# A planned order of steps, replanned from step 560 on: order, buffers and the engines of 50 steps

## The chip, the cores and the metric

One core of a Trainium2 chip runs the whole program. The metric is the device time of one execution in microseconds (us), as the median of three runs. The engines are named as in the profile: PE (matrix products), PEld (PE's weight loads, which overlap the products), DVE (vector engine), ACT (scalar engine), POOL (GpSimd) and SP (which issues the transfers).

## The reference, cut to what matters

```python
# q, k, v: (4, 4, 1088, 32); S1, S2: (8, 32); w1, w2: (128, 1024); w3: (1024, 1024); w_out: (1024, 128)
phi(x) = outer product of (S1 x) and (S2 x), 64 features for each position
kv  = einsum('bhsf,bhsd->bhfd', phi(k), v);  z = sum over s of phi(k)
att = einsum('bhsf,bhfd->bhsd', phi(q), kv) / (einsum('bhsf,bhf->bhs', phi(q), z) + 1e-6)
x   = att, heads side by side: (4352, 128)
out = ((x @ w1) * (x @ w2)) @ w3 @ w_out
```

## The kernel before, in words

The kernel is written as 1181 named steps, each a few instructions on one engine. A list, `ORDER`, gives the order in which they are issued; every engine works its own instructions off strictly in that order. Four further tables belong to the plan: `SLOTS` says which of the buffers of a kind each allocation takes (kind "b" is the eight PSUM banks; "l", "m" and "s" are SBUF buffers of three sizes; "raw" are the three biggest), `POOL` names the elementwise steps that run on POOL and not on DVE (the function `on`), `CPV` the copies that run on DVE and not on ACT (the function `cp`).

What the step names mean:

- `k0.*` to `k3.*`: the four batches of keys; `k3.kv*` are the value sums of the last batch that is taken up, of which the step that closes them is `k3.kvr`. `k2.kv*` are those of the third batch.
- `q0.*` to `q3.*`: half batches of 512 queries of batches 0 and 1. `q4.*` and `q6.*`: the 1024 queries of batches 2 and 3, as one chain each (`q_wide`, L1308 and below). `qr.*`: the 64 last positions of every batch. A chain runs `tr max l2 l1 rm A0 C0 C1 At Ct sm st sh sl sc al p01 p2 p12 dn de rc bs na nb nm nr ne nn phi pT x xT`. `phi0` and `phi1` (L1509) are the two halves of the feature product, 128x1024 each; `pT0` and `pT1` (L1517) turn them; `x` (L1527) is PE's product of the turned features with the key sums, 32 small products that write four PSUM banks; `xT0` to `xT3` (L1540) copy these banks out.
- `w*` and `f*`: the weights are unpacked, and w3 and w_out are folded into one matrix `w3o` (L534).
- `g0.*` to `g3.*`: the feed-forward layers for batches 0 and 1, eight slices each: `a` and `b` (L1799, L1809) are products with w1 and w2, `c` copies `a` out, `m` (L1815) multiplies, `o` (L1835) is the product with `w3o`. `oT` (L1842) takes the output bank out, `st` issues the transfers to the output.
- `h4.*` and `h6.*`: the feed-forward layers for batches 2 and 3, in which seven half-size products replace eight (`seven`, L1636 and below). For each of four slices and two halves `a`, `b`: `1` to `7` (L1673) are the products, `c d e i` (L1680) copies, `f g h` (L1685) sums with a bank. `m11 m12 m22` (L1707) and `m21` (L1712) multiply, `T1` to `T4` (L1727 to L1742) form differences, `P1` to `P7` (L1759) are the second products, `k1` to `k9` (L1767 to L1785) join them. `s1` to `s4` and `v.*`, `o.*` form the sums of the inputs and of the weights that these products need.
- `gr.*`: the feed-forward layer for the 256 left-over positions, PE L1799, L1809 and L1824.

Around the change the order was: while PE works through the `o` products of `g0` to `g3`, which depend on nothing that is still to come, DVE, POOL and ACT carry the chains `q4`, `q6` and `qr`; PE takes up `q4.x`, `q6.x` and `qr.x` between these products. Then come `h4`, `h6` and `gr`, whose products each wait for buffers and results of the other engines.

The rule by which a step finds its engine and its buffer:

```python
    def on(name):
        return pool if name in POOL else act if name in ACTS else dve

    def cp(name):
        return dve.tensor_copy if name in CPV else act.copy
...
        if tag in taken:
            return pool.tile(shape, dtype, tag=f"{tag}.{next(taken[tag])}", bufs=1, name=name)
```

Of the kernel before, what the change touches and what calls it, by code (L numbers as in the profile page):

```python
# [45 lines left out]

# [64 lines left out]
g3.5b q6.sl w10.a1 q6.sc q4.dn qr.At g3.5c q4.de f5.t q4.rc g1.0o g1.1o q4.na q4.bs q4.nb f2.m q4.nm q4.nr qr.sm q6.al
q6.p01 q6.p2 g0.0o g0.1o q6.p12 f2.o g0.2o g0.6o k2.kqt g0.3o q4.ne g3.5m q4.nn q6.dn k2.kq f5.m f5.o g3.7b g3.2b
g1.6o g0.5o g0.4o w10.a0 qr.st f7.t f7.m g3.2a q4.phi0 q4.phi1 qr.sh qr.sl qr.sc f7.o q4.pT0 g3.2c q4.pT1 g2.5o g0.7o
g0.oT g3.2m g3.3o g2.3o q4.x q4.xT2 q6.de qr.p01 q6.rc q4.xT0 q6.bs q6.nb q6.na g2.2o g2.7o qr.al q6.nm q6.nr q6.ne
q6.nn v.1 q4.xT1 q6.phi0 q6.phi1 g1.4o o.S3 q4.xT3 g1.2o q6.pT0 g3.5o g3.7m q6.pT1 g1.3o q6.x qr.p2 q6.xT2 qr.p12
qr.dn qr.de g3.1o g1.7o g3.6o g2.1o qr.rc qr.bs q6.xT3 g1.5o q6.xT0 h4.s1 h4.s3 q6.xT1 q6.ns g3.7o g3.2o qr.phi0
qr.pT0 g1.oT qr.x h4.0b5 h4.0a1 qr.xT0 h4.1a1 g2.oT g2.st h4.0b2 g3.oT h4.0a5 h4.0b1 h4.0bd h4.1b1 h4.0ac h4.s2 h4.s4
h4.1ac v.2 h4.0a6 h4.0bc h4.0bh h4.0ae o.S1 h6.s1 h4.0a2 h4.0ah h4.0b3 h4.1b2 o.S2 o.S4 h4.0ad h4.1a6 h6.s2 h4.0a7
h4.0m11 h4.0b6 h4.1a5 g3.st h4.1bc h4.1b6 h4.1ae h4.1bh v.4 h4.0ag h4.0be h4.0bf h4.1b5 h4.0a3 h4.0af h4.0b7 h4.1a7
h4.1be h4.1b7 h4.1ad h4.0a4 h4.0m12 h4.1a2 h4.0bg h4.1bd h4.1b3 h4.1a3 h4.0m22 h4.0b4 h4.1ag h4.2b1 h4.0ai h4.2a1  # L120
h4.1bf h4.2bc h4.2b2 h4.1ah h4.1a4 h4.2a2 h4.2ac h4.1bg h4.1af h4.1m12 h4.1m22 h4.1b4 h4.3b1 h4.2a6 h4.1ai h4.0m21
g1.st h4.2b5 h4.2ae h4.3a1 h4.2bh h4.1m11 h4.2ah h4.1m21 h4.3bc h4.1T1 h4.2m11 h4.3ac h4.2b6 h4.2be h4.2bd h4.0T1
h4.2a5 h4.2ad h4.3a2 h4.3b2 h4.3bh h4.3b6 h4.2a7 h4.2b7 h4.0T3 h4.3a6 h4.3ae h4.2ag h4.2b3 h4.3ah h4.3be h4.2a3 h4.3a5
h4.3ad h4.3b5 h4.3bd h4.2bg h4.2a4 h4.3b7 h4.3a7 h4.1T3 h4.2af h6.1b1 h4.2bf h4.3m11 h4.3a3 h4.2m22 h4.3bg h4.2b4
h4.2ai h4.3ag h4.2m12 h4.3b3 h6.0a1 h4.2m21 h6.0ac h4.3af h4.3a4 h4.1T2 h6.1bc h4.3b4 h6.1a1 h6.0b1 h6.0a6 h4.3ai
h4.3m21 h6.1b6 h4.3bf h4.2T1 h6.1ac h4.0P7 h4.2P1 h4.1P7 h4.0T2 h4.0P1 h4.0T4 h4.1P2 h4.3T1 h4.3m22 h4.1P5 h4.0P4
h6.0bc h4.2P2 h4.0P2 h4.3P5 h4.3m12 h4.2P5 h4.1P6 h4.2T2 h4.2P6 h4.0P5 h4.2T3 h4.1P1 h4.3T3 h4.3P7 h4.2P7 h4.3P1
h4.3T2 h4.3T4 h4.3P6 h4.2T4 h4.2P4 h6.0ae h4.0P6 h4.3P4 h4.1T4 h6.s3 h4.1P4 h4.k1 h4.k3 h4.3P2 h4.k2 h4.0P3 h4.3P3
h4.2P3 h4.k4 h4.k7 h4.1P3 h6.1be h4.k5 gr.1a h6.0b6 gr.1c h6.0be h6.0a7 h6.0b5 h6.0a5 h6.1a6 h6.0ad h6.1b7 h4.k8 h6.s4
h6.0a3 h6.0b7 h4.k6 h4.k9 g4.oT h6.0bd h6.0b3 h6.1a5 h6.0ag h6.0bg h6.0af q4.ns g4.oS h6.0b2 h6.0a4 h6.1a2 h6.1ae  # L130
h6.0bf h6.0b4 h6.1a7 h6.1b5 h6.0m12 h6.0bh h6.1b2 h6.0ai h6.0a2 h6.1ah h6.0m21 h6.2a1 h6.3b1 h6.1ad h6.1ag h6.1bd
h6.1a4 h6.1b3 h6.1bh h6.3bc h6.2ac h6.1ai h6.2b1 h6.0ah h6.1a3 h6.2a6 g4.st h6.2bc h6.2ae h6.1bg h6.1b4 h6.2a5 h6.2ad
h6.2b5 h6.1bf h6.2b6 h6.2be h6.2a2 h6.0m22 h6.0m11 h6.1m21 g0.st h6.2b2 h6.1af h6.3a1 h6.2bd h6.1m11 h6.2bh h6.3ac
h6.2b3 h6.2ah h6.2a3 h6.2b7 h6.2a7 h6.3a5 h6.3b5 h6.3a6 h6.2af h6.3b6 h6.3b2 h6.2bf h6.2bg h6.3a2 h6.3bd h6.0T1 h6.3ae
h6.3b3 h6.2ag h6.3ad h6.1T1 h6.3ah h6.1m22 h6.3a3 h6.3be h6.3b7 h6.3bf h6.2a4 h6.3af h6.1T2 h6.3bg h6.3a7 h6.2b4
h6.2m11 gr.7a gr.3a gr.5a h6.3ag h6.2ai gr.3c gr.2b h6.2m12 gr.2a h6.3bh h6.0T2 gr.7c gr.3b h6.1m12 h6.2m21 h6.0T4
gr.7b h6.3a4 h6.2T1 h6.3b4 h6.1P2 h6.0T3 h6.2m22 gr.5c h6.2T2 h6.3m11 gr.2c h6.1P5 h6.2P5 h6.2P1 gr.3m h6.3ai h6.3m21
h6.2T3 h6.3T1 h6.0P1 h6.0P7 h6.3m22 h6.3T2 h6.3T3 h6.0P5 h6.3P1 h6.1T3 h6.2P6 h6.0P4 h6.0P6 h6.2T4 gr.7m h6.2P4 h6.3P5
h6.1T4 h6.1P6 h6.2P7 h6.3P6 h6.1P1 h6.1P7 h6.3m12 h6.2P2 h6.3P7 h6.3P2 h6.3T4 h6.1P4 h6.0P2 h6.3P4 h6.k1 h6.0P3 h6.2P3
h6.1P3 h6.3P3 gr.2m g5.oT gr.3o1 gr.7o0 gr.7o1 g5.oS h6.k3 gr.2o0 h6.k2 gr.2o1 h6.k4 h6.k5 gr.5b h6.k7 gr.3o0 gr.6a  # L140
# [1794 lines left out]
```

## Time and profile before

| | us |
|---|---|
| three runs | 250.13, 250.77, 249.65; median 250.13 |
| the profiled execution | 248.89 |
| its span, first to last instruction | 246.9 |
| PE busy | 238.4 |
| DVE busy | 212.2 |
| POOL busy | 154.4 |
| ACT busy | 121.8 |

The span is what the trace covers; the 1.99 us between it and the execution's time lie around it. The profiled execution is 1.24 us below the median. A row of a view gives start, duration, engine, line of the code, operation, what is written and what is read, and in brackets how long the engine sat idle ahead of it and what ended that. Step 560, from which on the plan is new, falls at about 103.4 us of the span.

### The profile page before, as it was taken

Reading aid. Unit: us, or ns where it says so; the run is one execution under the profiler, and the core shown is the slowest. Engines: PE = TensorE matmul, PEld = TensorE weight load, DVE = VectorE, ACT = ScalarE, POOL = GpSimd, SP = SyncE. Lnnn points to the kernel's source line nnn. Section 1 sums busy time; section 2 is a strip of 40 time slices with the busy share of each in tenths; the row PEclk is TensorE's granted clock in tenths of the full one; section 3 lists DMA queues with packets and bytes.
Section 4 is the critical chain, followed back from the end, with each engine's and each line's share of the span. In section 5 each row is a group of like instructions: output and inputs, shape, how many; then the busy total and the mean of one; then the engine's idle time right before and its main releaser. Section 6 shows DMA issues by size and latency. Waiting matters only on the chain.

```text
span 246.9 us, 6753 instructions
## 1 busy us (share of the span) xinstructions
PE 238.4 (97%) x2726; PEld 133.7 (54%) x2726; DVE 212.2 (86%) x426; ACT 121.8 (49%) x246; POOL 154.4 (63%) x198
## 2 busy tenths in 40 slices
PE   8999999999999999999999988999999999999994
PEld 6887464554445556856666434447653344463373
DVE  2787989988999889889899888588999699799892
...
GB/s 202 267 167 324 173 204 185 92 229 135 244 177 230 183 230 142 3 4 0 3 0 0 3 1 3 54 73 4 0 0 0 3 11 74 1 0 3 0 53 96
DMA packets 31934, 22.06 MB, mean 89 GB/s; under 512 B 21280, under 2 KB 26528, under 8 KB 31904
## 3 DMA queue, kind: packets, MB, share of 16 engines
...
## 4 chain that ended last, share of the span: by engine, by line
PE 80%; DVE 15%; issue 2%; POOL 1%; ACT 0%; DVEq 0%
PE ps_X L1673 11%; PE ps_o L1759 10%; PE a_ps L1799 9%; PE b_ps L1809 9%; PE ps_o L1835 9%; PE ps_w3o L534 6%; PE ps_Y L1673 6%; PE idle_ps L255 4%; PE ps_Z L1673 3%; DVE ab L1815 3%; PE ps_g L659 2%; PE ps_ac L1374 2%; PE ps_kv L769 2%; PE ps_or L1824 2%; DVE pT L1517 1%
## 5 line engine op out<-in xcount | busy, mean ns | idle before, releaser
L1809 PE MATMUL b_ps<-xT,w 128*128 128x512 f32 (+1 forms) x80 | 36.4, 560 | 0.3 <-DVE ab L1815 0.2
L1673 PE MATMUL ps_X<-xd,wv 64*128 64x512 f32 x112 | 35.6, 595 | 0.0
L1799 PE MATMUL a_ps<-xT,w 128*128 128x512 f32 (+1 forms) x80 | 35.4, 558 | 0.0
L1804 ACT COPY ffa<-a_ps 128x512 f32<-128x512 f32 (+1 forms) x34 | 17.6, 536 | 30.4 <-PE a_ps L1799 30.3
L1680 ACT COPY hc<-ps_X 128x512 f32<-128x512 f32 x37 | 20.7, 589 | 21.2 <-PE ps_X L1673 12.9
L1835 PE MATMUL ps_o<-ab,w3o 128*128 128x512 f32 x64 | 29.4, 597 | 0.0
L1815 DVE TENSOR_TENSOR ab<-ffa,b_ps 128x512 f32<-128x512 f32 (+1 forms) x40 | 23.9, 619 | 3.2 <-PE b_ps L1809 2.5
L501 POOL TENSOR_TENSOR w3c<-w3c,cv_m 128x512 int32<-128x512 int32 x16 | 21.0, 1328 | 6.3 <-DVE w3c L495 6.3
L1799 PEld LDWEIGHTS a_ps<-xT,w 128*128 128x128 f32 x80 | 14.4, 190 | 14.6 <-issue 8.5
L1707 POOL TENSOR_TENSOR hc<-hc 128x512 f32<-128x512 f32 x15 | 19.7, 1327 | 2.9 <-DVE hc L1685 2.9
L1673 PEld LDWEIGHTS ps_X<-xd,wv 64*128 64x128 f32 x112 | 15.2, 186 | 10.4 <-issue 8.3
L1809 PEld LDWEIGHTS b_ps<-xT,w 128*128 128x128 f32 x80 | 14.0, 190 | 12.2 <-issue 7.7
L1673 PE MATMUL ps_Y<-xd,wv 64*128 64x512 f32 x48 | 19.2, 599 | 0.0
L1835 PEld LDWEIGHTS ps_o<-ab,w3o 128*128 128x128 f32 x64 | 11.7, 190 | 13.7 <-issue 13.2
L534 PEld LDWEIGHTS ps_w3o<-wo,w3T 128*128 128x128 f32 x128 | 15.3, 192 | 3.2 <-issue 2.5
L534 PE MATMUL ps_w3o<-wo,w3T 128*128 128x128 f32 x128 | 15.9, 277 | 0.6 <-DVE w3T L528 0.6
L1540 ACT COPY xd<-ps_x 64x256 f32<-64x256 f32 x32 | 11.7, 367 | 7.6 <-PE ps_x L1527 7.2
L538 ACT COPY w3o<-ps_w3o 128x128 f32<-128x128 f32 x8 | 2.0, 270 | 26.3 <-PE ps_w3o L534 26.3
L1759 PE MATMUL ps_o<-hc,w3o 128*64 128x512 f32 x32 | 14.7, 596 | 0.0
L1848 POOL TENSOR_TENSOR oT<-oT,nz 128x512 f32<-128x512 f32 x4 | 4.2, 1049 | 15.6 <-DVE oT L1842 14.4
L263 ACT ACTIVATE cv_c<-raw 128x1024 f32<-128x1024 f32 (+1 forms) x13 | 13.0, 1010 | 1.5 <-DMA raw<-in_moe_w_dram 1.5
L1509 POOL TENSOR_TENSOR ph<-s_al,s_bs 128x1024 f32<-128x1024 f32 x5 | 10.4, 2096 | 4.6 <-issue 4.5
...
## 6 DMA issues: line engine op xcount, KB each, us to landing
...
```

Source lines behind the costliest of these rows:

```text
L263: act.activation(dst, hi.bitcast(F32), ACT.Prelu, scale=2.0 ** -112, alpha=-2.0 ** 32)
L501: pool.tensor_tensor(d, d, x["m"][:, i * 512:(i + 1) * 512], ALU.add)
L534: pe.matmul(t["o"], w3T[ko][:, c], wo[:, c], start=c == 0, stop=c == NC - 1)
L1673: pe.matmul(x[bank], stat(j, u)[:, i * 128:(i + 1) * 128], rows(j, u), start=new, stop=True, tile_position=(u * 64, 0), skip_group_check=True)
L1680: cp(n(y))(x[k], x[bank])
L1707: on(f"h{g}.{i}m{k}").tensor_mul(both[0][k], both[0][k], both[1][k])
L1759: pe.matmul(acc_o[bank][half[0]:half[1]], w(i), x(i), start=n == 1, stop=n == (2 if j == 3 else 4), tile_position=(0, half[0]), skip_group ...
L1799: pe.matmul(x["a"][:, :w], w_of(0, c), xT[g][:, c0:c0 + w], start=True, stop=True)
L1804: cp(f"g{g}.{c}{su}c")(x["s"][:, :w], x["a"][:, :w])
L1809: pe.matmul(x["b"][:, :w], w_of(1, c), xT[g][:, c0:c0 + w], start=True, stop=True)
L1815: dve.tensor_mul(ab_sb[g, c][:, c0:c0 + w], x["s"][:, :w], x["b"][:, :w])
L1835: pe.matmul(o_ps[g], w3o[:, c], ab_sb[g, c], start=n == 1, stop=n == NC)
```

## The change

The set of 1181 steps and their code stay; the first 560 entries of `ORDER` stay. Of the other 621 the order is new, and with it the buffers from there on. 37 steps change their engine:

- from DVE to POOL (24): `h4.1T2 h4.1m22 h4.2T1 h4.2T4 h4.3m22 h4.s1 h4.s4 h6.0T3 h6.0m11 h6.1T3 h6.2T2 h6.2T3 h6.3T2 q4.al q4.bs q4.p01 q6.bs q6.p01 q6.p2 qr.al qr.bs qr.p2 qr.sc qr.sl`
- from POOL to DVE (13): `g7.oS h4.0m11 h4.1T3 h4.1m12 h4.2m11 h4.2m12 h4.3T4 h4.s2 h6.0T4 h6.0m22 h6.1T1 h6.2m11 q4.phi0`
- copies from DVE to ACT (7): `g3.4c h4.0ae h4.1ac h4.2ad h4.k1 h6.2bd h6.3ae`; from ACT to DVE (6): `h4.1bd h4.3ae h6.3bc h6.3be q6.xT0 q6.xT3`

(`h6.3ae` and the like are single copies of 128x512; `q6.xT0` and `q6.xT3` are four copies of 64x256 each.) With these 13 copies it is 50 steps whose engine is another.

The diff of the tables, cut to its form:

```diff
 SLOTS = {
     "b": 
         "012345670214657210671306537457462512346127340273051427362045726105341607575417607603461360"
-        "327725301236471236074513407615234072154607256037541641412037521403176043176027631701306317"
+        "327725301236471236074513407615234072154607256037541641412735401325167246105745016140145015"
...
-    "raw": "012012021020121",
+    "raw": "012012021021221",
...
 ORDER = """
...
-g3.1m w4.c w4.j k3.kv0 k3.kv1 k3.kv3 k3.kv2 k3.kvr q4.Ct q4.sm q6.l1 qr.max k3.kvc k2.kv1 k2.kv2 k2.kvr k2.kvc f3.m
...
+g3.1m w4.c w4.j k3.kv0 k3.kv1 k3.kv3 k3.kv2 k3.kvr q4.Ct qr.max q4.sm k3.kvc f0.o q6.l1 k2.kv1 k2.kv2 k2.kvr q4.st
...
```

What that moves is seen where the engines' instructions stand in a row. The after-kernel has one line more ahead of the steps, so its line numbers are one higher.

On PE, the stretch in which the products of the chains `q4`, `q6` and `qr` stand between the feed-forward products. `ps_x` with 32x256 is a product of `q4.x` (first group) or `q6.x` (second), `ps_x` with 32x64 one of `qr.x`; `ps_o` is an `o` product. Before:

```order
L1835 MATMUL ps_o<-ab,w3o 128x512 x3
L534 MATMUL ps_w3o<-wo,w3T 128x128 x8
L1799 MATMUL a_ps<-xT,w_81 128x512
L1835 MATMUL ps_o<-ab,w3o 128x512 x4
L1527 MATMUL ps_x<-pT,kq_2286 32x256 x32
L1835 MATMUL ps_o<-ab,w3o 128x512 x6
L1527 MATMUL ps_x<-pT,kq_2149 32x256 x32
L1835 MATMUL ps_o<-ab,w3o 128x512 x7
L1527 MATMUL ps_x<-pT,kq_659 32x64
```

On PE, the same place of the changed kernel:

```order
L1800 MATMUL a_ps<-xT,w_81 128x512
L1810 MATMUL b_ps<-xT,w_81 128x512
L1836 MATMUL ps_o<-ab,w3o 128x512 x3
L1528 MATMUL ps_x<-pT,kq_2166 32x256 x32
L1836 MATMUL ps_o<-ab,w3o 128x512 x8
L1528 MATMUL ps_x<-pT,kq_2079 32x256 x32
L1836 MATMUL ps_o<-ab,w3o 128x512 x12
L1528 MATMUL ps_x<-pT,kq_659 32x64
```

Both wide products stand earlier: twelve and no longer seven `o` products are left for the time behind `q6.x`. Counted over the whole stretch, `q4.x` has eight `o` products fewer ahead of it and one more (`g3.6o`); `q6.x` has eight fewer and three more. From the first product of `h4` on the same products are left in both kernels.

On DVE, the steps ahead of `q4.x`. `s_hl` and `s_pr` are buffers of the chains, `ph` and `pT` their features and turned features, `s_bs` and `s_al` the factors of the feature product, `ab` the result of an `m` step. Before (`qr.st`, `f7.t`, `qr.sh`, `qr.sl`, `qr.sc`, `q4.pT0` with `q4.pT1`, `g0.oT`, `g3.2m`):

```order
L201 SCALAR_TENSOR_TENSOR s_t_2306<-s_g,ay_A 128x128
L528 STREAM_TRANSPOSE w3T<-w3c 128x1024
L204 SCALAR_TENSOR_TENSOR s_hl<-s_g,s_t_2306 128x128
L1417 TENSOR_TENSOR s_hl<-ay_A,s_hl 128x128
L1421 TENSOR_TENSOR s_hl<-s_hl,ay_C 128x128
L1517 STREAM_TRANSPOSE pT<-ph 128x1024 x2
L1842 STREAM_TRANSPOSE oT<-ps_o 128x512
L1815 TENSOR_TENSOR ab<-ffa,b_ps 128x512
```

On DVE, the changed kernel there (`q4.ne`, `qr.sh`, `q4.phi0`, `q4.pT0`, `g3.7m`, `q4.pT1`, `g3.2m` with `g3.5m`, `q6.dn`):

```order
L1486 TENSOR_SCALAR nz<-nz 128x8
L205 SCALAR_TENSOR_TENSOR s_hl<-s_g,s_t_2289 128x128
L1510 TENSOR_TENSOR ph<-s_al,s_bs 128x1024
L1518 STREAM_TRANSPOSE pT<-ph 128x1024
L1816 TENSOR_TENSOR ab<-ffa,b_ps 128x512
L1518 STREAM_TRANSPOSE pT<-ph 128x1024
L1816 TENSOR_TENSOR ab<-ffa,b_ps 128x512 x2
L1446 TENSOR_REDUCE s_d<-s_pr 128x64
```

One of the two feature products of `q4` now stands in DVE's row, ahead of the transposes; the sums of `qr` have gone to POOL; three `m` steps stand ahead of `q6.dn` where one followed the transposes. In the changed kernel `q4.x` waits for the last of these, `g3.5m`, since it writes a bank that this step reads.

On POOL, the row in which `q4.phi0` and `q4.phi1` stood one after the other (`q6.p12`, `q4.nn`, `w10.a0`, both `phi`, `qr.p01`):

```order
L1440 TENSOR_TENSOR s_pr<-s_pr 128x256
L1490 TENSOR_TENSOR s_bs<-s_bs,nz 128x256
L501 TENSOR_TENSOR w3c<-w3c,cv_m 128x512
L1509 TENSOR_TENSOR ph<-s_al,s_bs 128x1024 x2
L1432 TENSOR_TENSOR s_pr<-s_hl 128x128
```

On POOL in the changed kernel (`q6.sc`, `q4.bs`, `q6.p01`, `q4.nn`, `q4.phi1`, `qr.sl`, `q6.al`, `qr.sc`, `q6.p2`, `q6.p12`):

```order
L1422 TENSOR_TENSOR s_hl<-s_hl,ay_C 128x512
L1460 TENSOR_TENSOR s_bs<-ay_C,s_rc 128x256
L1433 TENSOR_TENSOR s_pr<-s_hl 128x512
L1491 TENSOR_TENSOR s_bs<-s_bs,nz 128x256
L1510 TENSOR_TENSOR ph<-s_al,s_bs 128x1024
L1418 TENSOR_TENSOR s_hl<-ay_A,s_hl 128x128
L1427 TENSOR_TENSOR s_al<-s_hl 128x256
L1422 TENSOR_TENSOR s_hl<-s_hl,ay_C 128x128
L1437 TENSOR_TENSOR s_pr<-s_al,s_hl 128x256
L1441 TENSOR_TENSOR s_pr<-s_pr 128x256
```

One `phi` is left there, and `q4.bs`, `q6.p01`, `qr.sl`, `qr.sc` and `q6.p2` have come in around it.

On PE, the end of the program: the last second products of `h6` (`ps_o` from `hc` with `ws`) and the products of `gr` (`a_ps`, `b_ps`, `ps_or`). Before:

```order
L1759 MATMUL ps_o<-hc,ws 64x512 x4
L1824 MATMUL ps_or<-w3o,ab 128x128 x5
L1809 MATMUL b_ps<-xT,w_81 128x256
L1824 MATMUL ps_or<-w3o,ab 128x128
L1799 MATMUL a_ps<-xT,w_81 128x256 x3
L1809 MATMUL b_ps<-xT,w_81 128x256 x4
L1824 MATMUL ps_or<-w3o,ab 128x128 x10
```

On PE, the end of the changed kernel:

```order
L1810 MATMUL b_ps<-xT,w_81 128x256 x2
L1800 MATMUL a_ps<-xT,w_81 128x256
L1825 MATMUL ps_or<-w3o,ab 128x128 x3
L1760 MATMUL ps_o<-hc,ws 64x512 x2
L1825 MATMUL ps_or<-w3o,ab 128x128
L1800 MATMUL a_ps<-xT,w_81 128x256
L1810 MATMUL b_ps<-xT,w_81 128x256
L1800 MATMUL a_ps<-xT,w_81 128x256
L1825 MATMUL ps_or<-w3o,ab 128x128
L1810 MATMUL b_ps<-xT,w_81 128x256
L1825 MATMUL ps_or<-w3o,ab 128x128 x5
L1810 MATMUL b_ps<-xT,w_81 128x256
```

The kinds of product alternate more often there; counted from step 560 on, PE's row has 35 groups of one kind of product before and 40 now (second products of `h`, first products of `h`, feed-forward, left-over `a` and `b`, left-over `o`, folding, small products).

More of the change, by code (lines that the diff above doesn't have):

```diff
@@ L111 @@
[L111 to L140, printed above, removed]
@@ new lines @@
+q4.al q4.p2 g2.4o g3.3m g3.3o q6.Ct k2.kqt w10.m q6.sm k2.kq f1.o q6.st qr.A0 w8.a0 q6.sh qr.C0 qr.C1 q6.sl qr.Ct
+g0.0o f5.t w10.a0 qr.At qr.sm q4.p12 q4.dn f2.m w10.a1 q6.sc g0.1o g3.7b q4.de q4.rc q4.na q4.bs g3.2a f5.m f7.t g1.0o
+f5.o q4.nb q4.nm f7.m q4.nr q6.p01 f7.o qr.st f2.o q4.ne qr.sh g2.5o g3.2b q4.nn q4.phi0 q4.phi1 g0.2o g3.2c g3.5a
+q4.pT0 g3.7m g3.5b qr.sl g3.6o g0.6o q6.al q4.pT1 qr.sc g3.2m q6.p2 q6.p12 g3.5c g2.3o qr.al g3.5m q4.x q6.dn q6.de
+q6.rc g2.7o q6.na q6.bs q6.nb g0.5o q6.nm g0.4o g0.3o qr.p01 q4.xT0 q6.nr q6.ne q6.nn g3.7o q4.xT1 q6.phi0 q6.pT0
```

68 lines of the change are left out of this document (47 added, 21 removed).

## The prediction

> **What bounds the kernel now.** The page's busy line and its slices come first, then the chain that ended last (shares by engine), then three stretches of the part that is planned anew.
>
> ```profile
> PE 238.4 (97%) x2726; PEld 133.7 (54%) x2726; DVE 212.2 (86%) x426; ACT 121.8 (49%) x246; POOL 154.4 (63%) x198
> PE   8999999999999999999999988999999999999994
> PE 80%; DVE 15%; issue 2%; POOL 1%; ACT 0%; DVEq 0%
> core 0: us, PE busy (x) PEld busy (x) DVE busy (x) ACT busy (x) POOL busy (x), PEclk, DMA share, GB/s
> 103.00:158.00 55.00, 53.52 (x572) 29.62 (x561) 48.42 (x94) 22.01 (x53) 34.56 (x44) 1.00 0.01 3
> 158.00:235.00 77.00, 76.96 (x350) 36.34 (x352) 68.85 (x111) 29.76 (x59) 52.11 (x55) 1.00 0.10 18
> 235.00:246.90 11.90, 8.24 (x52) 6.53 (x48) 7.07 (x14) 1.29 (x4) 2.10 (x2) 1.00 0.39 72
> ```
>
> PE is the bound: 97% of the span, and 76.96 of 77.00 us in the stretch of `h4`, `h6` and most of `gr`. The set of products is the same after the change, so the time can move in three ways only: idle time of PE that goes or comes, products that run slower because their kinds alternate, and the end behind the last product. The first stretch holds 1.48 us of idle time, and DVE is busy for 48.42 of 55 us there. The visible stall is at the small products of the chains:
>
> ```profile
> 140.47 1.50 PE L1527 MATMUL ps_x<-pT,kq 32*32 32x256 f32 x64
> 141.90 5.42 PE L1835 MATMUL ps_o<-ab,w3o 128*128 128x512 f32 x12
> 148.41 0.76 PE L1527 MATMUL ps_x<-pT,kq 32*32 32x256 f32 x16 [1.09 <-DVE ab L1815]
> 149.56 1.36 PE L1527 MATMUL ps_x<-pT,kq 32*32 32x256 f32 x48 [0.39 <-DVE pT L1517]
> 143.29 0.19 PEld L1835 LDWEIGHTS ps_o<-ab,w3o 128*128 128x128 f32 x1 [0.24 <-issue]
> 143.72 0.19 PEld L1835 LDWEIGHTS ps_o<-ab,w3o 128*128 128x128 f32 x1 [0.24 <-issue]
> ```
>
> `q4.x` takes 141.90 − 140.47 = 1.43 us and nothing holds it up. `q6.x` could have started at 148.41 − 1.09 = 147.32 and ended at 148.75; it ended at 149.56 + 1.36 = 150.92. That is a loss of 2.17 us. Weight loads follow each other by 143.72 − 143.29 = 0.43 us; an `o` product makes two of them, 0.86 us.
>
> **The change part by part.**
>
> *q4.x, moved ahead.* Eight `o` products fewer and one more (`g3.6o`) stand ahead of it: PE arrives 7 × 0.86 = 6.0 us earlier, at 140.47 − 6.0 = 134.5. What it waits for stands on DVE: `q4.pT1` and then `g3.2m` and `g3.5m`. The rows on DVE and beside it on POOL:
>
> ```profile
> 135.74 2.37 DVE L1517 STREAM_TRANSPOSE pT<-ph 128x1024 f32<-128x1024 f32 x2
> 140.67 0.42 DVE L1459 TENSOR_TENSOR s_bs<-ay_C,s_rc 128x256 f32<-128x256 f32 x1
> 135.53 0.29 DVE L1421 TENSOR_TENSOR s_hl<-s_hl,ay_C 128x128 f32<-128x128 f32 x1
> L1707 DVE TENSOR_TENSOR hc<-hc 128x512 f32<-128x512 f32 x9 | 6.2, 692 | 0.0
> L1445 DVE TENSOR_REDUCE s_d<-s_pr 128x64 f32<-128x512 f32 x2 | 1.4, 679 | 0.0
> 139.50 0.65 DVE L1815 TENSOR_TENSOR ab<-ffa,b_ps 128x512 f32<-128x512 f32 x1
> 125.54 1.10 DVE L1459 TENSOR_TENSOR s_bs<-ay_C,s_rc 128x256 f32<-128x256 f32 x1
> 125.08 1.28 POOL L1421 TENSOR_TENSOR s_hl<-s_hl,ay_C 128x512 f32<-128x512 f32 x1
> 133.57 1.93 DVE L1417 TENSOR_TENSOR s_hl<-ay_A,s_hl 128x128 f32<-128x128 f32 x1
> 131.38 3.96 POOL L1509 TENSOR_TENSOR ph<-s_al,s_bs 128x1024 f32<-128x1024 f32 x2
> ```
>
> Before, the second transpose ended at 135.74 + 2.37 = 138.1. Nine steps leave DVE ahead of this point: `g3.4c`, `q4.p01`, `q6.p01` and `q6.dn` at 0.67 to 0.69 each, `q4.al`, `q4.bs` and `q6.p2` at 0.42, `qr.sl` and `qr.sc` at 0.29; together 4.6 us. Two of them also ran stretched beside POOL: `q4.bs` took 1.10 us where `q6.bs` of the same shape took 0.42, and `qr.sl` 1.93 where `qr.sc` took 0.29. These extra 0.68 + 1.64 = 2.3 us go as well. What comes in is `q4.phi0` and two `m` steps (0.65 each; `g3.5m` only moves behind the transposes). `q4.phi0` is the costly one:
>
> ```profile
> 143.57 2.86 DVE L1509 TENSOR_TENSOR ph<-s_al,s_bs 128x1024 f32<-128x1024 f32 x1 [0.30 <-DVE s_bs L1490]
> 143.40 1.95 POOL L1509 TENSOR_TENSOR ph<-s_al,s_bs 128x1024 f32<-128x1024 f32 x1 [4.47 <-issue]
> L677 DVE TENSOR_TENSOR kp<-kab x1: 1206/1206/1206, 16.6 to 16.6; 128x1024 f32<-128x1024 f32 x1
> ```
>
> Such a product with two SBUF inputs takes DVE 1.21 us by itself (`kp`, the features of the keys: min, median and max in ns, first and last start); beside POOL's half of the same features `q6.phi0` took 2.86 us: it ended 1.1 us after POOL's half (145.35), as if it had begun only then. After the change both halves of `q4` are released by one step, `q4.nn` on POOL, and POOL goes straight on to `phi1`, so I take 2.86. Bounds for it are these two rows, 1.21 and 2.86.
>
> Sum: 138.1 − 4.6 − 2.3 + 2 × 0.65 + 2.86 = 135.4. With 1.21 for `q4.phi0` it would be 133.7; with one more step stretched like `q4.bs` 136.1. I take 135.2, near the row of the pair, since POOL and DVE start the two halves together: `q4.x` is held up by **0.7 us** (0 to 1.6), where it was held up by nothing.
>
> By the Trainium skill, "SBUF — State Buffer", section "Who interferes with whom", a DVE instruction with two inputs in SBUF and a GpSimd instruction that reads SBUF contend for a shared port: whichever starts first holds it for its whole length, and the other is shut out. This speaks against putting `q4.phi0` beside `q4.phi1`. The rows above agree (2.86 against 1.21, 1.93 against 0.29). If the rule did not hold here, `q4.x` would be ready at 133.7, ahead of PE, and this term would be nothing.
>
> *q6.x, moved ahead.* Eight `o` products fewer and three more: 5 × 0.86 = 4.3 us, so PE arrives at 147.32 − 4.3 + 0.7 = 143.7. On DVE, `g3.7m` no longer stands between `q6.pT0` and `q6.pT1`, nor `q6.bs` and `qr.al` ahead of them. Before, the small steps from `q6.de` on began at 140.07 and `q6.phi0` at 143.57:
>
> ```profile
> 140.07 0.17 DVE L1450 SCALAR_TENSOR_TENSOR s_rc<-s_d 128x32 f32<-128x32 f32 x1
> 141.79 0.22 DVE L1426 TENSOR_TENSOR s_al<-s_hl 128x64 f32<-128x64 f32 x1
> 146.54 1.25 DVE L1517 STREAM_TRANSPOSE pT<-ph 128x1024 f32<-128x1024 f32 x1
> 148.28 1.23 DVE L1517 STREAM_TRANSPOSE pT<-ph 128x1024 f32<-128x1024 f32 x1
> ```
>
> From the end of `g3.5m` at 135.2: `q6.dn` 0.6, the small steps 3.50 − 0.42 − 0.22 = 2.9, `phi0` to the start of `pT0` 2.97, two transposes 2.4: 144.1. Some of the small steps have two SBUF inputs and now meet POOL's steps of `qr` and `q6.p2`; I add 0.4 (between nothing and the 0.68 that `q4.bs` was stretched by): 144.5. `q6.x` ended 150.92 − 149.51 = 1.4 after `pT1` before, so now at 145.9, against 143.7 + 1.43 = 145.1 without a stall: 0.8 us lost, where 2.17 were. Term: **−1.4 us**, bounds −2.2 (no stall) and 0.
>
> The copies of the banks of `q6.x` go to ACT (0.367 us each, 16 in a row) and stand ahead of nothing that PE needs before `h6`.
>
> ```profile
> L1540 ACT COPY xd<-ps_x 64x256 f32<-64x256 f32 x32 | 11.7, 367 | 7.6 <-PE ps_x L1527 7.2
> 157.06 0.92 PE L1527 MATMUL ps_x<-pT,kq 32*32 32x64 f32 x64
> ```
>
> *qr.x and the start of h4.* Twelve `o` products (10.3 us) follow `q6.x`, so PE comes to `qr.x` at 145.9 + 10.3 = 156.2, or 156.3 with the switch of the next part, 0.8 earlier than the row above. What `qr.x` needs is moved forward with the rest of DVE's row, since five of `qr`'s steps leave DVE. I cost the wait at nothing; its cover is the last of these `o` products, and one step of DVE that POOL holds up (0.68) would cost no more than that.
>
> *Kinds of product that alternate.* At a switch the loads were apart by 142.43 − 141.90 = 0.53 instead of 0.43:
>
> ```profile
> 141.90 0.30 PEld L1835 LDWEIGHTS ps_o<-ab,w3o 128*128 128x128 f32 x2 [0.41 <-issue]
> 142.43 0.19 PEld L1835 LDWEIGHTS ps_o<-ab,w3o 128*128 128x128 f32 x1 [0.24 <-issue]
> ```
>
> PE's row has 40 groups of one kind instead of 35: 5 × 0.10 = **+0.5 us** (bounds 0 and 1).
>
> *h4, h6 and gr.* Here PE waited for nothing before. Of the steps of `h` 13 go from DVE to POOL and 11 the other way, on the same tiles of 128x512:
>
> ```profile
> L1707 POOL TENSOR_TENSOR hc<-hc 128x512 f32<-128x512 f32 x15 | 19.7, 1327 | 2.9 <-DVE hc L1685 2.9
> 190.32 1.28 DVE L1742 TENSOR_TENSOR tt<-tt,hc 128x512 f32<-128x512 f32 x2
> 190.47 2.86 POOL L1742 TENSOR_TENSOR tt<-tt,hc 128x512 f32<-128x512 f32 x1 [4.95 <-DVE tt L1732]
> 224.04 1.66 POOL L1742 TENSOR_TENSOR tt<-tt,hc 128x512 f32<-128x512 f32 x1 [3.56 <-DVE tt L1732]
> ```
>
> A step costs POOL 1.33 us where DVE takes 0.69, and a POOL step that met DVE's two-input steps took 2.86. Net, POOL gets two steps more. Laid out in these durations, the results of `h4` come 0.2 to 0.35 us ahead of PE (an estimate from the rows above), so that PE still works through. In the last slices of `h6` the change gives POOL `2T2` and `3T2` beside `2T3` and `2T4`; the second products `2P4` to `3P7` need them, and by the same estimate they come between 1 us early and 1 us late. I take **+0.2** (0 to 1 in the forecast; more is a rival). A copy that goes from DVE to ACT, or back, is hidden: ACT is busy 29.76 of 77 us there.
>
> *The end.* The last products are those of `gr` in both kernels, and their output takes the same way:
>
> ```profile
> 241.74 1.50 PE L1824 MATMUL ps_or<-w3o,ab 128*128 128x128 f32 x12
> 243.68 0.62 SPq L1562 DMA_DIRECT2D out_dram<-oT  x1
> ```
>
> Span 246.9 less 243.68 is the transfer's 3.2 us; nothing is to be gained or lost there.
>
> **Sum.** +0.7 − 1.4 + 0.5 + 0.2 = 0.0 us. Against the profiled execution, 248.89 us (span 246.9 and 1.99 around it), that is 248.9; the median of the runs, 250.13, lies 1.24 above that execution, so the forecast for the median is **250.1 us**.
>
> **Rivals.**
>
> 1. *Both stalls go (faster).* If DVE is early by more than I count (134.5 in the lower sum) and `q4.phi0` doesn't meet `phi1` in full, neither product waits: −2.17, with 0.5 for the switches 248.5 us. For it: five DVE steps of `qr` and three each of `q4` and `q6` go to POOL, and 2.3 us of stretching with them. Against: `phi0` and `phi1` have one releaser, and that is the very pair that took 2.86 in `q6`. Chance 0.20.
> 2. *The last slices of h6 wait for POOL (slower).* A POOL step that DVE's two-input steps shut out took 2.86 instead of 1.33, 1.5 more. Three of the four POOL steps `2T2`, `3T2`, `2T3`, `2T4` delaying the second products by about 0.8 each beyond their margin give +2.4: 252.5 us. It decides once a wait is above the margin of 0.3 to 0.9 us. For it: POOL gets two steps more in the halves (2 × 1.33 = 2.7 us), and the row at 190.47 shows the shut-out. Against: the row at 224.04, only 0.33 above 1.33. Chance 0.22.
> 3. *More stretching ahead of q4.x (slower).* POOL's new `q4.bs`, `q6.p01`, `qr.sl`, `q6.p2` meet DVE's `p12`, `de`, `nm`: two more steps stretched like `q4.bs` (0.68 each) hold both wide products up by 1.4: 251.5 us. Chance 0.10.
>
> That the order doesn't change what it says is excluded by the rows above: the two wide products do stand 7 and 5 products earlier.
>
> **How the numbers follow.** Forecast 0.48, rivals 0.20, 0.22, 0.10. A measurement of this kernel can tell about 0.5% (1.25 us) from no change: below 248.88 is faster, above 251.38 slower. Faster 0.20 (most of rival 1, a little of the forecast), slower 0.32 (rival 2, half of 3 and a little of the forecast's upper end), same 0.48. The range goes from rival 1's 248.4 to just past rival 2's 252.5: 248.4 to 252.7.
>
> **What would show it.** `q4.x` at about 135 with some 0.7 us of idle time ahead of it, ended by DVE's `ab`; a DVE row of 2.9 us for `q4.phi0` with a POOL row of 2.0 beside it; `q6.x` from about 143.7, with one wait of under 1 us for `pT`; the first product of `h4` near 157.2 where it was near 158.0. POOL rows above 1.6 us after 215 with idle time of PE behind them would be rival 2. No idle time at either wide product would be rival 1. The forecast is wrong if the stretch of `h4` and `h6` holds more than 1.5 us of idle time, or if PE's products there run at another pace than 0.43 us a load.

## The result, and the profile after

The changed kernel takes 249.43 us (median of 22 runs, 248.34 to 251.17), the kernel before 249.53 us in the same comparison (22 runs, 248.22 to 251.22): ratio 1.000, 95% interval 0.998 to 1.002. No difference can be measured. The profiled execution of the changed kernel spans 247.3 us, that of before 246.9.

The rows of the changed kernel's page that answer to those shown of before:

```profile
PE 238.8 (97%) x2726; PEld 131.4 (53%) x2726; DVE 211.1 (85%) x420; ACT 120.7 (49%) x241; POOL 163.7 (66%) x209
PE 59%; DVE 26%; POOL 6%; issue 4%; ACT 3%; DVEq 0%; POOLq 0%; ACTq 0%
```

and its three stretches, with the same columns as before:

```profile
103.00:158.00 55.00, 54.27 (x589) 30.09 (x580) 46.48 (x91) 19.60 (x47) 42.74 (x41) 1.00 0.01 2
158.00:235.00 77.00, 76.60 (x347) 33.98 (x344) 69.47 (x107) 30.66 (x57) 54.77 (x70) 1.00 0.11 19
235.00:247.30 12.30, 8.63 (x52) 6.50 (x51) 7.85 (x15) 1.38 (x4) 1.05 (x1) 1.00 0.35 64
```

The chain that ended last now runs through DVE and POOL for 32% of the span, where it was 16%: PE is held by them at more places. In the first stretch PE is idle 0.73 us where it was 1.48; in the second 0.40 where it was 0.04. The sum hides larger moves. PE's rows in which it waited, and the products of the chains:

```profile
116.31 1.12 PE L1836 MATMUL ps_o<-ab,w3o 128*128 128x512 f32 x2 [0.29 <-DVE ab L1816]
135.23 1.50 PE L1528 MATMUL ps_x<-pT,kq 32*32 32x256 f32 x64
143.73 1.50 PE L1528 MATMUL ps_x<-pT,kq 32*32 32x256 f32 x64
155.93 0.27 PE L1528 MATMUL ps_x<-pT,kq 32*32 32x64 f32 x2 [0.20 <-DVE pT L1518]
156.44 0.84 PE L1528 MATMUL ps_x<-pT,kq 32*32 32x64 f32 x62 [0.24 <-DVE oT L1843]
182.03 0.69 PE L1674 MATMUL ps_X<-xd,w 64*128 64x512 f32 x1 [0.34 <-DVE hc L1686]
```

Neither wide product waits: the 2.17 us lost at `q6.x` are gone. In their place stand three waits that before did not have: at `g3.3o` (116.31), at `qr.x` (155.93 and 156.44), and at `h6.1a1` (182.03).

The table gives PE's time between marks of its own row, in us, for the two kernels and for the runs told of below. The first mark is `k3.kvr`, the last product of the steps that are the same in both (103.06 in the profile of before, 103.28 in that of the changed kernel).

| kernel | to q4.x | to q6.x | to h4 | h4 to gr.1a | gr.1a to P of h6 | to the last product's end | sum |
|---|---|---|---|---|---|---|---|
| before | 37.41 | 45.35 | 54.85 | 39.21 | 26.26 | 19.86 | 140.18 |
| changed | 31.95 | 40.45 | 53.92 | 39.78 | 26.49 | 20.29 | 140.48 |
| raw_before | 37.41 | 44.19 | 53.03 | 39.20 | 25.96 | 19.87 | 138.06 |
| v1_late | 31.95 | 40.45 | 53.16 | 39.66 | 26.49 | 20.28 | 139.59 |
| mended | 31.39 | 39.90 | 52.60 | 39.66 | 26.51 | 20.28 | 139.05 |
| mended_tail | 31.40 | 39.89 | 52.60 | 39.67 | 25.95 | 19.86 | 138.08 |

From the first to the second row: `h4` starts 0.93 earlier, and 0.57 + 0.23 + 0.43 = 1.23 are given back behind it. The difference of the sums, 0.30, less 0.12 that the end behind the last product got shorter, is 0.18 us.

Why the wait at `q6.x` is gone stands in the rows of the two halves of its features, DVE's and POOL's, in the changed kernel:

```profile
128.56 1.23 DVE L1510 TENSOR_TENSOR ph<-s_al,s_bs 128x1024 f32<-128x1024 f32 x1 [0.60 <-POOL s_bs L1491]
128.60 3.00 POOL L1510 TENSOR_TENSOR ph<-s_al,s_bs 128x1024 f32<-128x1024 f32 x1
139.03 1.22 DVE L1510 TENSOR_TENSOR ph<-s_al,s_bs 128x1024 f32<-128x1024 f32 x1
139.22 2.85 POOL L1510 TENSOR_TENSOR ph<-s_al,s_bs 128x1024 f32<-128x1024 f32 x1 [1.65 <-issue]
```

The first pair is `q4`'s, the second `q6`'s. Before, DVE's half took 2.86 and POOL's 1.95; now DVE's takes 1.2 and POOL's about 2.9. In each pair the one that starts first, here DVE by 0.04 and 0.19 us, runs at its own length.

### The profile page after: what moved, and what is told of

It reads as the page before. It is cut to its first block, busy times and chain, and to the rows that moved or that the text cites. A ratio compares the mean times of both kernels' runs of the same rounds, so it can differ in the third digit from the quotient of the medians.

```text
span 247.3 us, 6776 instructions
## 1 busy us (share of the span) xinstructions
PE 238.8 (97%) x2726; PEld 131.4 (53%) x2726; DVE 211.1 (85%) x420; ACT 120.7 (49%) x241; POOL 163.7 (66%) x209
## 4 chain that ended last, share of the span: by engine, by line
PE 59%; DVE 26%; POOL 6%; issue 4%; ACT 3%; DVEq 0%; POOLq 0%; ACTq 0%
PE ps_o L1760 8%; PE a_ps L1800 8%; PE b_ps L1810 7%; PE ps_X L1674 6%; PE ps_w3o L535 5%; PE idle_ps L256 3%; PE ps_o L1836 3%; DVE ab L1816 3%; PE ps_g L660 2%; ACT xd L1541 2%; PE ps_Y L1674 2%; DVE w3c L496 2%; DVE hc L1686 2%; PE ps_Z L1674 2%; PE ps_kv L770 2%
## 5 line engine op out<-in xcount | busy, mean ns | idle before, releaser
L1674 PE MATMUL ps_X<-xd,wv 64*128 64x512 f32 x112 | 39.8, 597 | 0.1
L1800 PE MATMUL a_ps<-xT,w 128*128 128x512 f32 (+1 forms) x80 | 35.9, 558 | 0.0
L1805 ACT COPY ffa<-a_ps 128x512 f32<-128x512 f32 (+1 forms) x35 | 18.4, 536 | 28.9 <-PE a_ps L1800 28.8
L1674 PEld LDWEIGHTS ps_X<-xd,wv 64*128 64x128 f32 x112 | 15.9, 186 | 11.4 <-issue 7.3
L1674 PE MATMUL ps_Y<-xd,wv 64*128 64x512 f32 x48 | 20.5, 597 | 0.0
L1708 POOL TENSOR_TENSOR hc<-hc 128x512 f32<-128x512 f32 x12 | 15.9, 1339 | 0.6 <-DVE hc L1686 0.5
L1541 ACT COPY xd<-ps_x 64x256 f32<-64x256 f32 x24 | 8.8, 367 | 8.3 <-PE ps_x L1528 6.7
L1760 PE MATMUL ps_o<-tt,ws 128*64 128x512 f32 x32 | 12.6, 597 | 0.0
L1733 POOL TENSOR_TENSOR tt<-hc,tt 128x512 f32<-128x512 f32 x6 | 8.3, 1400 | 5.3 <-DVE hc L1708 3.2
L1760 PE MATMUL ps_o<-hc,ws 128*64 128x512 f32 x32 | 11.7, 597 | 0.0
```

The source lines that it names most:

```text
L1541: eng(xd[key, t // 2][k][u * 64:u * 64 + 64, t % 2 * W:t % 2 * W + W], s["x"][t][k * 64:k * 64 + 64, :W])
L1674: pe.matmul(x[bank], stat(j, u)[:, i * 128:(i + 1) * 128], rows(j, u), start=new, stop=True, tile_position=(u * 64, 0), skip_group_check=True)
L1708: on(f"h{g}.{i}m{k}").tensor_mul(both[0][k], both[0][k], both[1][k])
L1760: pe.matmul(acc_o[bank][half[0]:half[1]], w(i), x(i), start=n == 1, stop=n == (2 if j == 3 else 4), tile_position=(0, half[0]), skip_group ...
L1800: pe.matmul(x["a"][:, :w], w_of(0, c), xT[g][:, c0:c0 + w], start=True, stop=True)
L1805: cp(f"g{g}.{c}{su}c")(x["s"][:, :w], x["a"][:, :w])
```

## The experiments

Ratios are to the kernel before, run beside on the same chip. Two theories were tried on the first question, why `q6.x` no longer waits. *First start*: the half that starts first shuts the other out, and the change altered which one that is. *Order*: the stall belonged to where the product stood.

**raw_before: one digit in the kernel before.** In `SLOTS`, `q6.phi0` takes the buffer that `q4` has done with, and not one that a transfer had filled:

```diff
-    "raw": "012012021020121",
+    "raw": "012012021020101",
```

> The kernel before with one digit of the buffer table changed: q6.phi0 takes the buffer of q4.phi0 (0) instead of buffer 2, whose last user was a transfer, so that fewer waits stand ahead of it on DVE. Theory 'first start': of the two feature halves, DVE's and POOL's, the one that starts first runs at its own length and shuts the other out; before, DVE's half started 0.17 us after POOL's only because of the extra waits. Expected: DVE's half 1.2 us and POOL's about 2.9 instead of 2.86 and 1.95, q6.pT1 ends near 147.5 (was 149.5), loss at q6.x 0 to 0.7 us (was 2.17), first product of h4 near 156.3 to 156.9 (was 157.9), time 1.0 to 2.0 us below before. Rival 'order': the stall at q6.x belongs to where the product stands in PE's row, the buffer is nothing; time within 0.5 us of before, DVE's half stays at 2.9.

246.92 us against 249.23: ratio 0.990 (0.987 to 0.993), 2.3 us faster. The waits that DVE's queue works off for this line, in before and in this run (min, median and max in ns, first and last start):

```profile
L1509 DVEq EVENT_SEMAPHORE  x4: 21/50/50, 142.9 to 143.5; - x4
```

```profile
L1509 DVEq EVENT_SEMAPHORE  x2: 21/36/50, 143.1 to 143.1; - x2
```

and the two halves in this run, first DVE's, then POOL's, with PE's product:

```profile
143.59 1.23 DVE L1509 TENSOR_TENSOR ph<-s_al,s_bs 128x1024 f32<-128x1024 f32 x1
```

```profile
143.63 3.00 POOL L1509 TENSOR_TENSOR ph<-s_al,s_bs 128x1024 f32<-128x1024 f32 x1 [4.48 <-DVE s_bs L1490]
```

```profile
147.46 1.87 PE L1527 MATMUL ps_x<-pT,kq 32*32 32x256 f32 x64
```

With two waits fewer DVE starts 0.04 ahead of POOL, where it started 0.17 behind. The half takes 1.23, the second transpose ends at 147.9 in place of 149.5, and the product starts without an idle time, with no product moved; it takes 1.87 and not 1.50, so that about 0.4 of the 2.17 us are still lost. The gain of 2.3 us is a little more than the 1.0 to 2.0 that were expected: `h4` starts 1.82 us earlier than before, where the whole change brought 0.93, and 0.30 more are gained between `gr.1a` and the second products of `h6`. *Order* is refuted as a need: the stall goes with the order of before.

**raw_flip: the reverse, in the changed kernel.** `q4.pT0` takes buffer 0, so that `q6.phi0` is again the first user behind a transfer:

```diff
-    "raw": "012012021021221",
+    "raw": "012012021021021",
```

> The changed kernel with one digit of the buffer table changed: q4.pT0 takes buffer 0, so that q6.phi0 is again the first user of buffer 2 after a transfer, as before the change. 'First start': POOL's half of q6 starts first, 1.95 us, DVE's takes 2.9; q6.pT1 ends near 144.5 (was 143.4) and q6.x waits 0.7 to 1.1 us, as the prediction had it; POOL is free 0.9 us earlier for qr's steps, so qr.x waits less and h4 starts 0 to 0.5 us later; time 0 to 0.5 us above the changed kernel. 'Order': nothing changes, q6.x has no wait.

249.38 us, ratio 0.999 (0.996 to 1.001). The turn did not come about: DVE's half still began first, and no time between two marks moved by more than 0.04 us. So the run does not tell the theories apart.

```profile
L1510 DVEq EVENT_SEMAPHORE  x2: 50/50/50, 140.5 to 140.6; - x2
140.44 0.42 DVE L1491 TENSOR_TENSOR s_bs<-s_bs,nz 128x256 f32<-128x256 f32 x1
140.90 1.23 DVE L1510 TENSOR_TENSOR ph<-s_al,s_bs 128x1024 f32<-128x1024 f32 x1
141.00 2.94 POOL L1510 TENSOR_TENSOR ph<-s_al,s_bs 128x1024 f32<-128x1024 f32 x1 [1.57 <-issue]
```

The digit did bring two waits ahead of DVE's half, where the changed kernel has none. But DVE's queue worked both off while the step ahead, `q6.nn` (140.44 to 140.87), still ran, and the half began 0.03 us behind that step, as in the changed kernel. In the kernel before, the last two of the four waits came only after `q6.nn` had ended at 143.27 (at 143.38 and 143.48). As far as these rows show, it is not the number of waits that decides, but whether any are left when the step ahead has ended.

**small_ahead and small_behind: who starts first, forced.** Two steps of 0.2 us are put on DVE, once between `q6.nn` and `q6.phi0`, once behind `q6.phi0` (two digits of the small buffers in `SLOTS` change places with them):

```diff
-    ... qr.al qr.bs qr.p01 qr.p12 qr.p2 qr.sc ...
+    ... qr.bs qr.p01 qr.p12 qr.sc ...
...
-q6.nn g3.7o q4.xT1 q6.phi0 q6.pT0
+q6.nn g3.7o q4.xT1 qr.al qr.p2 q6.phi0 q6.pT0
```

and for small_behind, with the same change of `POOL`:

```diff
-q6.nn g3.7o q4.xT1 q6.phi0 q6.pT0
+q6.nn g3.7o q4.xT1 q6.phi0 qr.al qr.p2 q6.pT0
```

> The changed kernel with two small steps of the left-over chain, qr.al and qr.p2 (128x64, about 0.2 us each), put from POOL to DVE and placed there between q6.nn and q6.phi0, so that DVE begins its half of the features 0.4 us later than it did (139.03) and POOL (139.22) begins first. 'First start': POOL's half 1.95 us, DVE's 2.6 to 2.9, ending near 142.4; both transposes follow, q6.pT1 ends near 144.8 (was 143.4) and q6.x loses 0.7 to 1.2 us (was nothing). 'Order, not the port': DVE's half stays at 1.2 us and all on DVE comes 0.4 us later, no loss at q6.x.

> The control of the run before: the same two steps on DVE, placed behind q6.phi0. 'First start': DVE still begins first, 1.2 us against POOL's 2.9; q6.pT1 within 0.2 us of the changed kernel, no loss at q6.x. 'Order, not the port': the same as in the run before, within 0.4 us.

In small_ahead, POOL starts at 139.70 and DVE at 139.79, and the lengths change places:

```profile
139.65 0.22 DVE L1437 TENSOR_TENSOR s_pr<-s_al,s_hl 128x64 f32<-128x64 f32 x1
139.79 2.98 DVE L1510 TENSOR_TENSOR ph<-s_al,s_bs 128x1024 f32<-128x1024 f32 x1
142.80 2.37 DVE L1518 STREAM_TRANSPOSE pT<-ph 128x1024 f32<-128x1024 f32 x2
```

```profile
139.70 1.99 POOL L1510 TENSOR_TENSOR ph<-s_al,s_bs 128x1024 f32<-128x1024 f32 x1 [1.65 <-issue]
141.65 1.70 POOL L1614 TENSOR_TENSOR ws<-w3o 128x256 f32<-128x256 f32 x1
```

POOL's next step, 0.72 us long in the changed kernel, then takes 1.70 beside DVE's half. `q6.x` takes 2.31 us instead of 1.43, a loss of 0.9 within the expected 0.7 to 1.2, though only 0.4 us of work were added. Who is 0.09 us ahead decides over 1.75 us of length. In small_behind DVE starts first and its half takes 1.23, as expected, but the control went wrong behind it:

```profile
138.40 1.23 DVE L1510 TENSOR_TENSOR ph<-s_al,s_bs 128x1024 f32<-128x1024 f32 x1
139.54 1.98 DVE L1427 TENSOR_TENSOR s_al<-s_hl 128x64 f32<-128x64 f32 x1
141.55 0.65 DVE L1437 TENSOR_TENSOR s_pr<-s_al,s_hl 128x64 f32<-128x64 f32 x1
142.12 2.36 DVE L1518 STREAM_TRANSPOSE pT<-ph 128x1024 f32<-128x1024 f32 x2
```

```profile
138.58 2.86 POOL L1510 TENSOR_TENSOR ph<-s_al,s_bs 128x1024 f32<-128x1024 f32 x1 [1.65 <-issue]
```

`qr.al`, a step of 0.22 us with two inputs, met POOL's half under way (138.58 to 141.44) and took 1.98. Both transposes came behind it, and `q6.x` lost 0.4 + 0.9 us. The transpose itself is not held: in the changed kernel `q6.pT0` ran from 140.29 in 1.25 us beside that same POOL row. The times are 249.56 (ratio 1.002, 1.000 to 1.004) and 249.69 (1.002, 1.000 to 1.004): of the losses at `q6.x`, 0.9 and 1.3 us, only 0.13 and 0.55 are left at the first product of `h4` (54.05 and 54.47 from `k3.kvr`, 53.92 in the changed kernel), since `qr.x` then does not wait.

**phi0_pool: the step that the prediction priced highest, put back.**

```diff
-    ... q4.nn q4.p01 q4.p2 q4.phi1 ...
+    ... q4.nn q4.p01 q4.p2 q4.phi0 q4.phi1 ...
```

> The changed kernel with q4.phi0 back on POOL, where both halves of q4 then follow each other. The prediction priced DVE's half of q4 at 2.86 us; in the changed kernel it took 1.23 and POOL's 3.00. Theory 'first start, with slack': both halves on POOL take 2 x 1.97, end 0.9 us later than now (132.5), q4.pT1 ends near 133.8 (was 132.9), g3.5m waits for PE anyway, so q4.x starts as now; POOL's following steps come 0.9 later, q6.x loses 0 to 0.5 us; time 0 to 0.5 us above the changed kernel. Rival 'the engine of q4.phi0 is what the gain rests on': q4.x loses 0.7 us or more, time over 0.7 us above the changed kernel.

249.07 us, ratio 1.000 (0.999 to 1.002). `q4.x` starts at 31.95 and `q6.x` at 40.45 from `k3.kvr`, as in the changed kernel; `h4` starts 0.16 later. The reason is the wait of `g3.5m` in both: its buffer comes free only when PE has done an `o` product. First the changed kernel, then this run:

```profile
132.81 0.65 DVE L1816 TENSOR_TENSOR ab<-ffa,b_ps 128x512 f32<-128x512 f32 x1
134.55 0.69 DVE L1816 TENSOR_TENSOR ab<-ffa,b_ps 128x512 f32<-128x512 f32 x1 [1.09 <-PE ps_o L1836]
```

```profile
133.57 0.65 DVE L1816 TENSOR_TENSOR ab<-ffa,b_ps 128x512 f32<-128x512 f32 x1
134.47 0.69 DVE L1816 TENSOR_TENSOR ab<-ffa,b_ps 128x512 f32<-128x512 f32 x1 [0.25 <-PE ps_o L1836]
```

DVE had 1.09 us in hand at `q4.x`, so that the engine of `q4.phi0` decides nothing there.

**v1_late: where the first part gives back.** POOL's step `v.1` is moved behind `qr.bs`:

```diff
-qr.p2 v.1 qr.p12 qr.dn g1.7o qr.de qr.rc g2.2o g3.2o qr.bs g1.4o
+qr.p2 qr.p12 qr.dn g1.7o qr.de qr.rc g2.2o g3.2o qr.bs v.1 g1.4o
```

> The changed kernel with v.1 (two sums of weights on POOL, 2.5 us) moved behind qr.bs on POOL. Theory 'given back at qr': the gain at the wide products is given back at qr.x, where PE loses 0.7 us because POOL works v.1 off ahead of qr.p12. Expected: qr.dn on DVE near 144.9 (was 147.4), no wait at qr.x, first product of h4 near 156.5 (was 157.2), time 0.7 us below the changed kernel. Rival: qr.x waits just as long for its bank (g1.oT on DVE), or v.1 is then late for h4; time within 0.2.

248.74 us, ratio 0.997 (0.995 to 0.999); `h4` starts 0.76 earlier than in the changed kernel (53.16 for 53.92), and `qr.x` has no wait. The changed kernel itself did not run beside it, but raw_flip, whose marks are the same as its own, did: 249.38, which is 0.64 more. The rows of POOL in the changed kernel show what stood in the way:

```profile
144.11 0.32 POOL L1437 TENSOR_TENSOR s_pr<-s_al,s_hl 128x64 f32<-128x64 f32 x1
144.39 1.26 POOL L1584 TENSOR_TENSOR wv<-w 64x512 f32<-64x512 f32 x1
145.73 1.26 POOL L1585 TENSOR_TENSOR wv<-wv 64x512 f32<-64x512 f32 x1
147.07 0.32 POOL L1441 TENSOR_TENSOR s_pr<-s_pr 128x64 f32<-128x64 f32 x1
```

The first and the last are `qr.p2` and `qr.p12`; the two of `v.1` between them hold the left-over chain up by 2.7 us.

**front_after and rest_after: the two parts alone.** The first is the changed kernel up to the first product of `h4` and before from there; the second the reverse. Buffers are renamed to fit, and `POOL`, `CPV` go with the steps. The steps that only one kernel had issued by then go to the seam (front_after against the changed kernel, then rest_after against the kernel before):

```diff
-g1.oT g3.1o g0.7o g3.5o qr.x h4.0a5 g0.oT q6.xT1 h4.0b1 h4.0b5 ...
+g1.oT g3.1o g0.7o g3.5o qr.x v.3 g0.oT q6.xT1 q6.ns h4.0b5 h4.0a1 ...
```

```diff
-qr.phi0 qr.pT0 g1.oT qr.x h4.0b5 h4.0a1 qr.xT0 h4.1a1 ...
+qr.phi0 qr.pT0 g1.oT qr.x h4.s2 v.2 g2.oT h6.s1 h4.0a5 h4.0b1 ...
```

> The changed kernel up to the first product of h4, from there on the order, engines and buffers of the kernel before (buffers renamed so that they fit). Theory 'given back later': the first part gains 0.9 us, the rest loses 1.2 us (a wait at the start of h6, more switches between kinds of product). Expected: first product of h4 near 157.2, from there to the end as before (89.0 us), no idle time of PE in h4 and h6, time 0.7 to 1.0 us below before. Rival 'the first part gains nothing that lasts': time within 0.3 of before, since h4's other steps hold PE up when it comes earlier.

> The kernel before up to the first product of h4, from there on the order, engines and buffers of the changed kernel. 'Given back later': first product of h4 as before; from there to the last product 86.6 us where before has 85.3, with a wait of 0.5 us at the start of h6; time 0.8 to 1.5 us above before. Rival: the second part costs nothing by itself, its waits came only from starting earlier; time within 0.5 us of before.

249.41 us (0.999, 0.997 to 1.001) and 254.94 us (1.023, 1.020 to 1.026): both off, and both inconclusive as whole times, since the seam made waits of its own: from `h4` to `gr.1a` they take 40.64 and 44.75 us, where before has 39.21 and the changed kernel 39.78. PE waits for sums on POOL that neither kernel has so late; in front_after and in rest_after:

```profile
167.88 0.69 PE L1674 MATMUL ps_X<-xd,wv 64*128 64x512 f32 x1 [0.39 <-POOL wv L1600]
```

```profile
166.81 0.69 PE L1674 MATMUL ps_Y<-xd,w 64*128 64x512 f32 x1 [3.01 <-POOL xd L1660]
```

What can be read is what lies far from the seam. From `gr.1a` to the last product front_after takes 46.13 us, as before does (46.12). In rest_after the wait at `h6.1a1` is there though all comes later, and the last section takes 20.28 us, as in the changed kernel.

**mended: the three new waits taken away.** Beside `v.1`, POOL's `h4.0T3` goes behind `h6.s2`, and DVE's `g3.3m` ahead of `w10.j`:

```diff
-g3.7a w10.c g3.7c w10.j ... q4.al q4.p2 g2.4o g3.3m g3.3o
+g3.7a w10.c g3.7c g3.3m w10.j ... q4.al q4.p2 g2.4o g3.3o
...
-h4.0T3 h4.3b7 h4.3a7 h4.3m11 h4.2a3 h4.2bg h4.3b3 h6.s2 h4.2b4
+h4.3b7 h4.3a7 h4.3m11 h4.2a3 h4.2bg h4.3b3 h6.s2 h4.0T3 h4.2b4
```

> The changed kernel with three moves against its own new waits: v.1 behind qr.bs on POOL (0.7 us at qr.x), h4.0T3 behind h6.s2 on POOL, so that it no longer runs beside h4.3m11 on DVE (0.5 us at the start of h6), g3.3m ahead of w10.j on DVE (0.4 us at g3.3o). Theory 'given back in waits': the three waits go, time 1.3 to 1.6 us below the changed kernel and 1.0 to 1.6 below before. Rival 'the waits only move': under 0.8 us below the changed kernel.

247.53 us, ratio 0.994 (0.991 to 0.996), 1.7 us below before. The sum of the marks falls by 1.43 against the changed kernel: 0.56 ahead of `q4.x`, all of it at `g3.3o` (the product starts 0.46 earlier, and the next one follows it by 0.43 and not by 0.53), 0.76 at `qr.x`, and 0.12 between `h4` and `gr.1a`, where 0.5 was expected: the wait at `h6.1a1` went, and two smaller ones came up ahead of it. The move of `h4.0T3` brought nothing that the marks show, since v1_late, in which that step stays where it was, has the same 39.66 and no wait at `h6.1a1` either. The wait had come from the same contest as that of the two halves. DVE's `h4.3m11` and POOL's `h4.0T3` in the changed kernel, `h4.3m11` in this run, and the two in v1_late:

```profile
177.20 1.79 DVE L1708 TENSOR_TENSOR hc<-hc 128x512 f32<-128x512 f32 x1
```

```profile
177.17 1.27 POOL L1738 TENSOR_TENSOR hc<-hc 128x512 f32<-128x512 f32 x1
```

```profile
176.33 0.68 DVE L1708 TENSOR_TENSOR hc<-hc 128x512 f32<-128x512 f32 x1
```

```profile
177.50 0.68 DVE L1708 TENSOR_TENSOR hc<-hc 128x512 f32<-128x512 f32 x1
177.59 1.72 POOL L1738 TENSOR_TENSOR hc<-hc 128x512 f32<-128x512 f32 x1
```

In the changed kernel POOL was first by 0.03 us, and DVE's step took 1.79 instead of 0.68. In v1_late, with these two steps in the same order, DVE was first by 0.09 us: its step took 0.68, and POOL's 1.72 instead of 1.27. That turn was not planned: only `v.1` had been moved.

**mended_tail: the last third of before behind it.** `mended` up to `gr.1a`, before's order from there:

```diff
-h4.k5 h4.k7 h4.k6 h4.k8 gr.1a h6.s4 h4.k9 gr.1c h6.0a7 h6.0b6 ...
+h4.k5 h4.k7 h4.k6 h4.k8 q6.ns g1.st gr.1a h6.0b6 gr.1c h6.0be h6.0a7 ...
```

> The kernel 'mended' up to gr.1a (the first product between h4 and h6), from there on the order, engines and buffers of the kernel before (buffers renamed so that they fit). Theory 'given back in the last third': after gr.1a the changed order costs 0.6 us (more switches between kinds of product, the wait behind gr.1b). Expected: from gr.1a to the last product 46.1 us instead of 46.8, time 0.5 to 0.7 us below mended, 1.5 to 2.0 below before. Rival: what comes earlier waits at the end for DVE; within 0.2 us of mended.

247.26 us, ratio 0.993 (0.991 to 0.994). From `gr.1a` to the last product 45.81 us, where mended has 46.79: 0.98 less on PE's row, where 0.7 was expected; before itself takes 46.12 there, and raw_before gained the same 0.3 over it. In the medians it is 1.7 us below before, as mended was, so that what it adds to mended is not shown by the times. Both beat before. raw_before, the one digit, is as fast as mended_tail as far as can be told: the intervals of the ratios overlap (0.987 to 0.993 and 0.991 to 0.994), the sums of the marks are 138.06 and 138.08, and in both PE is busy for all of the 132.00 us from 103 to 235.

## Why the prediction was right

The forecast was no change, 0.0 us by the sum, and the ratio is 1.000. That the size came out is luck: the sum was 1.5 us too high at the wide products and 1.7 us too low elsewhere. (The 250.1 us of the forecast started from 250.13, the median of three runs of the kernel before; over 22 runs that kernel has 249.53.)

- *q4.x, +0.7.* Wrong. It starts with no wait, since DVE's half took 1.23 and not 2.86. The step that failed is "POOL and DVE start the two halves together", from which I took the longer row: DVE began 0.04 ahead, and then POOL is the one shut out. The lower sum, 133.7, was near the truth: without its wait for PE, `g3.5m` would have ended near 134.1 (133.46, the end of `g3.2m`, and 0.6). PE comes 5.46 us earlier and not 6.0, for the 0.56 lost at `g3.3o`; mended, without that wait, has 6.0. A lost start would have cost about 0.5 us (an estimate: 1.63 more for DVE's half, less the 1.09 that DVE had in hand), so the term hung on who began first.
- *q6.x, −1.4.* The direction was right, and the size −2.17: again DVE was first. Its half began at 139.03, where the terms gave 139.1, but not for the reason given. No small two-input step was stretched by POOL, for which I had added 0.4; instead DVE waited for `q6.bs`, which the change had moved to POOL:

```profile
137.19 0.42 DVE L218 TENSOR_REDUCE s_d<-s_bs 128x32 f32<-128x256 f32 x1 [0.46 <-POOL s_bs L1460]
```

- *qr.x, 0.* Wrong by 0.76. I had looked for the cover on PE and for DVE's load, and not at the queue of POOL, where `v.1` stood between two steps of the chain; v1_late shows it.
- *The start of h4.* Expected near 157.2, measured 157.20, again by luck: 1.5 us less than the sum were lost at the wide products, and 1.3 us that it did not have were lost at `g3.3o` and `qr.x`.
- *Switches, +0.5, and h4, h6 and gr, +0.2.* Together 0.7 expected, and 1.23 measured behind the start of `h4`: 0.57 up to `gr.1a`, and 0.66 from there on. The 0.66 go when before's order stands there (mended_tail); how much of them is switches and how much the wait behind `gr.1b` was not taken apart. The 0.57 are mis-sized against the 0.2, and their cause stays open: the one wait that the trace shows there, at `h6.1a1`, follows a DVE step that POOL shut out (177.20), but v1_late, without it, is only 0.12 shorter. That PE waited for nothing in this part before was also not quite so: by raw_before 0.30 us could be gained there.
- *The rivals.* The first came true in its mechanism, and its sign, no idle time at either wide product, is what the rows show; for its time 2.4 us are missing, which came up elsewhere: 0.56 + 0.76 + 0.57 + 0.23 + 0.43, less 0.12 at the end. (Its text puts the lower sum at 134.5; the lower sum is 133.7, and 134.5 is when PE was to arrive.) The second and third rival, with their times, are refuted: four POOL rows in the last slices of `h6` do take 1.66 to 1.73 us, but PE has no wait behind them, and none at either wide product.
